# One-core delta-rule, Mish and Sinkhorn-gated expert kernel: the queue order of the first expert's values, gating steps and token sums is rewritten

## The chip, the cores and the metric

The kernel runs on one core of a Trainium2 chip. The metric is the device time of one execution in microseconds (us), the median of the runs of a kernel. Five engines have instruction queues of their own and run them in order: PE (TensorE, matrix products into PSUM), DVE (VectorE), ACT (ScalarE), POOL (GpSimd) and SP (SyncE, which here issues every DMA). An instruction that has to wait holds up all that stands behind it on its engine.

## The reference, cut to what matters

Three stages follow each other. A delta-rule attention gives 3072 tokens of 384 values. A gated MLP (Mish) follows. The last stage, to which the change belongs, is a dense mixture of eight experts, whose gates `P` are normalised by eight Sinkhorn rounds over all tokens:

```python
logits = x @ w_gate
P = np.exp(logits - logits.max())
for _ in range(8):
    P /= P.sum(1, keepdims=True) + 1e-09
    P /= P.sum(0, keepdims=True) + 1e-09
    P *= N / E
for e in range(E):
    h = np.maximum(x @ w1[e], 0.0)
    out += P[:, e:e + 1] * (h @ w2[e])
```

## The kernel before, in words

**Two phases.** Phase 1 walks six blocks of 512 tokens and does attention, the MLP and expert 0 for each. Phase 2 does experts 1 to 7. Its unit is a pair (e, i, g): expert e, token block i (0 to 5), group g of 256 hidden units (0 to 3). There are 7 x 6 x 4 = 168 pairs; pair p = 0 to 23 are those of expert 1, the first in phase 2 ("the first expert" of the change). Values are split into a high and a low part, so each product is three matmuls.

**What a pair does.** `first(p)` (matmuls L487) forms seven small products of the 128x256 quarters of x and w1 (a Strassen-like scheme) in four PSUM tiles: `b0` and `b2` from a pool of two ("h"), `b1` and `b3` from another pool of two ("a"), 3, 9, 9 and 12 matmuls in this order. `evacuate(p)` combines them: ACT copies `b0` (L509), DVE adds (L510 to L513, out of `b1`, `b2`, `b2`, `b3`), ACT applies the ReLU (L514), DVE forms the low part (L515). `second(p)` (24 matmuls, L1348) multiplies by w2 and adds into four PSUM tiles `o`; after the fourth group DVE multiplies `o` by the gate and adds it to the token sums `acc` (L1353). PE's order is first(0), first(1), second(0), first(2), second(1) and so on, so one pair's evacuation has a whole pair of matmuls to hide behind. A PSUM tile is written again only when its last reader has finished: `b1` of pair p+1 takes the place of what used "a" two tiles ago.

**What is prepared beside it, in the pairs of expert 1.** (1) The values of the next token block: `x_fetch` brings them from DRAM into the one buffer `gxr` (SP, L449), `x_begin` forms the four differences that the scheme needs (DVE, L456 to L459), three `x_split` calls make the high part (ACT, L465) and the low part (POOL, L466) in one of two buffers `gx`, and `x_store` writes them to DRAM for the later experts (SP, L469, tile `xcd`, 2.3 MB). (2) The weights: `g_load` forms sums (DVE, L432 to L435) and splits (ACT L437, POOL L439), then has the next ones fetched (SP, L412 and L416). (3) The Sinkhorn rounds: a `sink_step` is half a round. `sink_round` is five DVE instructions (L353 to L357); `sink_round_end` is one matmul (L361) into a PSUM tile taken from the pool "a", and four DVE instructions (L363 to L366). Fourteen of the 22 steps run in phase 1; eight are left for phase 2. (4) The token sums: expert 0's result, which phase 1 left in DRAM (`y0d`), is loaded into `acc` (SP, L1369) and multiplied by expert 0's gate (DVE, L1407), four instructions for each block, which can only start when all Sinkhorn steps are done.

**What sets the order.** The order on each engine is that of the Python loop over p (L1374 to L1407): first, evacuate, two sink steps, second of the pair before, two sink steps, `g_load` at p = 1 and 5 in expert 1, then one piece of the next block's values (`x_begin` at g = 0, a split at g = 1, 2 and 3, with fetch, store and the load of the sums of block i + 2 behind the last split), and at the end two multiplications of token sums.

Of the kernel before, what the change touches and what calls it, by code (L numbers as in the profile page):

```python
# [13 lines left out]
ALU = mybir.AluOpType  # L14
# [70 lines left out]
def delta_mish_sinkhorn_kernel(  # L85
# [16 lines left out]
    nc = tc.nc  # L102
# [226 lines left out]
    P = lg  # L329
# [42 lines left out]
    def sink_step():  # L372
        if sinks:
            sinks.popleft()()
# [4 lines left out]
    NGR = U2 // 2  # L379
# [3 lines left out]
    order = list(range(NBLK))  # L383
# [60 lines left out]
    def x_fetch(i):  # L444
        if i >= NBLK:
            return
        c = order[i]
        r = pool2["xr"].tile([128, NX, 256], F32, tag="xr", name="gxr")
        nc.sync.dma_start(out=r[:, 0:6].rearrange("p a x -> p (a x)"), in_=x2_dram[c].rearrange("p k x -> p (k x)"))  # L449
        xraw[i] = r  # L450
# [11 lines left out]
    def x_split(i, k):  # L462
        r, x = xraw[i], xq[i]
        s = slice(3 * k, 3 * k + 3)
        nc.scalar.activation(out=x[:, 0, s], in_=r[:, s], func=AF.Copy)  # L465
        nc.gpsimd.tensor_tensor(out=x[:, 1, s], in0=r[:, s], in1=x[:, 0, s].bitcast(F32), op=ALU.subtract)  # L466

    def x_store(i):
        nc.sync.dma_start(out=xc_dram[order[i]], in_=xq[i].bitcast(F32))  # L469
# [8 lines left out]
    def first(p):  # L478
        e, i, g = pairs[p]
        w, x = gslots[gslot(p)], xq[i]  # L480

        def prod(ps, *terms):
            last = 3 * len(terms) - 1
            n = 0
            for a, b in terms:
                for pw, px in PASSES:
                    mm(ps, lhsT=w[:, pw, a * 128:a * 128 + 128], rhs=x[:, px, b, :], start=(n == 0), stop=(n == last))  # L487
                    n += 1

        b0 = ps_h.tile([128, 512], F32, tag="h", name="b0")  # L490
        prod(b0[:, 0:256], (0, 0))
        b1 = ps_a.tile([128, 512], F32, tag="a", name="b1")
        prod(b1[:, 256:512], (7, 7))
        prod(b1[:, 0:256], (2, 2), (4, 4))
        b2 = ps_h.tile([128, 512], F32, tag="h", name="b2")
        prod(b2[:, 0:256], (8, 8))
        prod(b2[:, 256:512], (6, 6), (5, 5))
        b3 = ps_a.tile([128, 512], F32, tag="a", name="b3")
        prod(b3[:, 0:256], (3, 1), (5, 4))
        prod(b3[:, 256:512], (1, 3), (9, 5))  # L500
        fbanks[p] = [b.rearrange("p (a x) -> p a x", a=2) for b in (b0, b1, b2, b3)]
# [25 lines left out]
    if True:  # L527
# [708 lines left out]
        with tc.manual_schedule():  # L1236
            banks[:] = [0, [A1, A1]]
            for c in range(NBLK):
                pe, rest, late = window(c)
                if c == NBLK - 1:  # L1240
                    p1.close()
                    open_second()
                    rest["s1"].append(g_fetch)
                    rest["s1"].append(lambda: x_fetch(0))
                    for f in (5, 9, 13):
                        rest[f"s{f}"].append(g_load)
                    rest["s7"].append(lambda: x_begin(0))
                    for k, f in enumerate((8, 10, 11)):
                        rest[f"s{f}"].append(lambda k=k: x_split(0, k))
                    rest["s15"].append(lambda: x_store(0))  # L1250
                    rest["s15"].append(lambda: x_fetch(1))
                m0 = PLACES[0][0]
                b = c * NU

                def side_pe(m, part):
                    return [st() for st in (pe[m][2:] + late[m] if part else pe[m][:2])]

                def side_rest(m, posts):
                    for p in posts:
                        p()  # L1260
                    for r in rest[m]:
                        r()
                    for p in side_pe(m, 1):
                        p()

                rate(0.4 if c == 0 else 0.6)
                for f in range(U1 + 3):
                    m = MARKS[f]
                    posts = side_pe(m, 0)
                    if f < U1:  # L1270
                        ready(b + f)
                        m_first(b + f)
                    if 1 <= f <= U1:
                        m_a(b + f - 1)
                        m_c(b + f - 1)
                    if not c and f < m0:
                        elim1(10, nc.gpsimd)
                    if f == 0 and c:
                        y0_second(b - 1)
                    if f == 1 and c:  # L1280
                        y0_done(c - 1)
                    if f == 2 or not c:
                        banks[1] = [A1, A1, (ps_o1, "o3")]
                    if f == U1 + 1:
                        m_second(b + U1 - 1)
                        x2_done(c)
                    side_rest(m, posts)
                    if 2 <= f <= U1:
                        m_second(b + f - 2)
                    fill(2.0)  # L1290
                    if f < U1:
                        if not c:
                            decodes(min(U1, f + 4))
                            converts(min(U1, f + 3))
                            begins(min(U1, f + 5))
                        if ncvt[0] >= U1:
                            conversions(b + f)
                side_rest("f4", side_pe("f4", 0))
                fill(2.0)
                banks[1] = [A1, A1]  # L1300
                for f in range(U1, NU):
                    u = b + f
                    posts = side_pe(f"s{f}", 0)
                    ready(u)
                    e_first(u, ps_h, mi_p, x1h, x1l)
                    if f > U1:
                        e_relu(u - 1)
                    side_rest(f"s{f}", posts)
                    if f > U1:
                        fill(3.6 if c == 0 else 3.2)  # L1310
                    if c == NBLK - 1 and f > U1:
                        sink_step()
                        sink_step()
                    if f > U1 + 1:
                        y0_second(u - 2)
                    conversions(u)
                e_relu(b + NU - 1)
                split = [lambda kc=kc: st_x1(c + 1, kc) for kc in range(KD)] if c + 1 < NBLK else []
                if split:
                    run(*split[0:2])  # L1320
                y0_second(b + NU - 2)
                if split:
                    run(split[2])
            y0_second(NBLK * NU - 1)
            y0_done(NBLK - 1)
# [36 lines left out]
    with tc.manual_schedule():  # L1362
        N = len(pairs)
        todo = deque((c, t) for c in order for t in range(4))

        def acc_load(i):
            if i < NBLK:
                have[0] = i + 1
                nc.sync.dma_start(out=acc[order[i]], in_=y0_dram[order[i]])  # L1369

        have = [0]

        acc_load(0)
        acc_load(1)  # L1374
        for p in range(N + 1):
            if p < N:
                e, i, g = pairs[p]
                first(p)
                evacuate(p)
                sink_step()  # L1380
                sink_step()
            if p >= 1:
                second(p - 1)
                sink_step()
                sink_step()
                if pairs[p - 1][1] == NBLK - 1 or p in (1, 5):
                    g_load()
            if p < N:
                if e == 1 and i + 1 < NBLK:
                    if g == 0:  # L1390
                        x_begin(i + 1)
                    elif g < NGR - 1:
                        x_split(i + 1, g - 1)
                    else:
                        x_split(i + 1, 2)
                        x_fetch(i + 2)
                        x_store(i + 1)
                        acc_load(i + 2)
                elif g == 0 and p + NGR < N:
                    x_load(p + NGR)  # L1400
            if not sinks and todo:
                for _ in range(2):
                    if not todo or order.index(todo[0][0]) >= have[0]:
                        break
                    c, t = todo.popleft()
                    a = acc[c][:, t, :]
                    nc.vector.tensor_scalar(out=a, in0=a, scalar1=P[:, 4 * c + t, 0:1], scalar2=None, op0=ALU.mult)  # L1407


# [61 lines left out]
```

## Time and profile before

| | |
|---|---|
| median of 3 runs | 2378.32 us (2370.19, 2378.47, 2378.32) |
| the profiled execution | 2370.12 us, its span 2368.3 us |
| PE busy | 2254.5 us, 95% of the span |
| DVE / ACT / POOL busy | 52% / 26% / 22% |
| mean granted clock of TensorE | 0.969 of full speed |
| phase 2 | from 950.2 us to the end, 168 pairs |

The span is the profile's time from the first instruction to the last; the execution's own time is 1.8 us longer. PE is busy nearly everywhere, so the places where it isn't are what a change of order can touch. Below, a line of a timeline reads: start in us, length in us, engine, line, instruction, output<-input, shapes, how many were merged, and in brackets the idle time before and what ended it.

### The profile page before, as it was taken

What the parts mean: (1) busy time and instruction counts of PE and PEld (TensorE: products, weight loads), DVE (VectorE), ACT (ScalarE), POOL (GpSimd) and SP (SyncE); (2) the same over time, 40 slices, a digit from 0 to 9 for tenths busy, and PEclk for the clock granted to TensorE, in tenths of its full rate; (3) what the DMA queues carried; (4) which work ended last, traced back from release to release, by engine and by line L of the source; (5) the groups of instructions that cost most, each with busy time, mean ns of one, the idle gap of its engine ahead of it and who ended that gap; (6) DMA issues with size and microseconds to landing.
All of it is one profiled execution on the core that took longest, in us unless ns stands there. A gap on an engine that the chain in (4) does not pass through costs nothing.

```text
span 2368.3 us, 41965 instructions
## 1 busy us (share of the span) xinstructions
PE 2254.5 (95%) x18012; PEld 2084.9 (88%) x18012; DVE 1236.1 (52%) x2009; ACT 619.7 (26%) x1012; POOL 529.4 (22%) x439
## 2 busy tenths in 40 slices
PE   6698899999999999897999999999999999999998
PEld 3477778888888878897999999999999999999998
DVE  8875725427172123764555555555555555555554
ACT  5244332333323232221321221121122122112111
POOL 5586441331412051131300020030020002002000
PEclk7799999999999999998999999999999999999999
DMA  5367643637344565332231232222213113221321
GB/s 173 114 208 219 206 150 130 207 121 241 132 151 164 173 230 195 121 105 109 108 143 45 81 134 81 80 86 89 81 67 145 47 77 133 81 80 68 107 84 51
DMA packets 74441, 297.04 MB, mean 125 GB/s; under 512 B 7504, under 2 KB 39504, under 8 KB 68880
## 3 DMA queue, kind: packets, MB, share of 16 engines
q1 hardware_dynamic: 74256, 294.36, 36.0%
q8 instruction: 142, 2.33, 0.4%
q14 instruction: 43, 0.35, 0.0%
HBM read 247.15 MB, written 47.19 MB: 124 GB/s over the span
## 4 chain that ended last, share of the span: by engine, by line
issue 35%; PE 10%; DMA 5%; POOL 4%; DVE 1%; SPq 0%; ACT 0%; POOLq 0%; DVEq 0%; ACTq 0%
PE o L1348 5%; PE b L487 5%; DMA gr<-in_w_dram 4%; POOL gw L439 2%; POOL gx L439 1%; DMA acc<-y0d 1%; SPq L412 0%; POOL gx L466 0%; DVE acc L1353 0%; ACT gh L514 0%; DVE gt L510 0%; DVE gt L513 0%; ACT gw L437 0%; DVE gt L511 0%; DVE acc L1407 0%
## 5 line engine op out<-in xcount | busy, mean ns | idle before, releaser
L487 PE MATMUL b<-gx,gw 128*128 128x256 f32 x3564 | 452.5, 284 | 17.7 <-DVE gt L510 12.4
L487 PEld LDWEIGHTS b<-gx,gw 128*128 128x128 f32 x3564 | 444.2, 192 | 22.5 <-DVE gt L510 14.1
L1348 PE MATMUL o<-gw,gh 128*128 128x384 f32 x1728 | 443.0, 337 | 2.1 <-DVE acc L1353 2.1
L514 ACT ACTIVATE gh<-gt 128x1024 fp32r<-128x1024 f32 x168 | 178.3, 1061 | 647.2 <-DVE gt L513 647.2
L1348 PEld LDWEIGHTS o<-gw,gh 128*128 128x128 f32 x1728 | 309.7, 190 | 2.6 <-issue 2.6
L296 PE MATMUL psh<-xh,w 128*128 128x512 f32 x864 | 289.0, 416 | 23.2 <-DMA w<-wd 12.9
L515 DVE SCALAR_TENSOR_TENSOR gl<-gt,gh 128x1024 fp32r<-128x1024 f32 x168 | 209.6, 1247 | 189.4 <-ACT gh L514 189.4
L1348 PE MATMUL o<-gw,gl 128*128 128x384 f32 x864 | 291.1, 337 | 0.0
L510 DVE TENSOR_TENSOR gt<-b,gt 128x512 f32<-128x512 f32 x168 | 116.2, 691 | 302.0 <-PE b L487 238.1
L1348 PE MATMUL o<-gx,gh 128*128 128x384 f32 x960 | 247.5, 339 | 2.4 <-DVE acc L1353 2.4
L487 PE MATMUL b<-gx,gx 128*128 128x256 f32 x1980 | 243.7, 280 | 0.8 <-ACT gt L509 0.6
L487 PEld LDWEIGHTS b<-gx,gx 128*128 128x128 f32 x1980 | 240.4, 188 | 2.2 <-ACT gt L509 1.2
L296 PEld LDWEIGHTS psh<-xh,w 128*128 128x128 f32 x864 | 160.8, 195 | 65.1 <-issue 19.1
L978 POOL TENSOR_TENSOR gl<-x,gh 128x512 fp32r<-128x512 f32 x96 | 128.7, 1340 | 394.1 <-ACT gh L977 393.8
L439 POOL TENSOR_TENSOR gw<-gr,gw 128x512 fp32r<-128x512 f32 x72 | 90.8, 1293 | 561.4 <-ACT gw L437 561.4
L296 PE MATMUL psh<-xl,w 128*128 128x512 f32 x432 | 176.0, 407 | 4.2 <-DVE xl L607 4.2
L1348 PEld LDWEIGHTS o<-gx,gh 128*128 128x128 f32 x960 | 171.6, 188 | 2.9 <-issue 2.0
L1348 PEld LDWEIGHTS o<-gw,gl 128*128 128x128 f32 x864 | 163.6, 189 | 0.4
L1348 PE MATMUL o<-gx,gl 128*128 128x384 f32 x480 | 162.7, 339 | 0.0
L509 ACT ACTIVATE gt<-b 128x256 f32<-128x256 f32 x168 | 64.2, 382 | 352.2 <-PE b L487 328.9
L989 PE MATMUL x<-gh,w 128*128 128x512 f32 x576 | 150.0, 396 | 0.0
L439 POOL TENSOR_TENSOR gx<-gr,gx 128x512 fp32r<-128x512 f32 x40 | 50.4, 1294 | 440.9 <-ACT gx L437 440.9
(182 smaller groups left out, 2992.2 us busy)
## 6 DMA issues: line engine op xcount, KB each, us to landing
w<-wd SPq DMA_DIRECT2D x120, 768.0 KB, 4.6
gx<-xcd SPq DMA_DIRECT2D x36, 2304.0 KB, 9.0
gr<-in_w_dram SPq DMA_DIRECT2D x56, 384.0 KB, 3.6
wd<-w SPq DMA_DIRECT2D x24, 768.0 KB, 4.7
xcd<-gx SPq DMA_DIRECT2D x6, 2304.0 KB, 11.0
kq<-in_qkb_dram SPq DMA_DIRECT2D x20, 256.0 KB, 7.0
vt<-in_vtok_dram SPq DMA_DIRECT2D x6, 768.0 KB, 8.3
kq<-in_w_in_dram SPq DMA_DIRECT2D x12, 384.0 KB, 4.7
```

The lines of the kernel that those rows point to most:

```text
L296: mm(ps, lhsT=wi(u, pw, kc), rhs=(xh, xl)[px][:, kc, :], start=(n == 0), stop=(n == 3 * KD - 1))
L439: nc.gpsimd.tensor_tensor(out=w[:, 1, q:q + 512], in0=r[:, q:q + 512], in1=w[:, 0, q:q + 512].bitcast(F32), op=ALU.subtract)
L487: mm(ps, lhsT=w[:, pw, a * 128:a * 128 + 128], rhs=x[:, px, b, :], start=(n == 0), stop=(n == last))
L509: nc.scalar.activation(out=t[:, 7], in_=b0[:, 0], func=AF.Copy)
L510: tt(out=t[:, 0:7:6], in0=b1, in1=t[:, 7:8].to_broadcast([128, 2, 256]), op=ALU.add)
L514: nc.scalar.activation(out=h, in_=t[:, 0:4], func=AF.Relu)
L515: nc.vector.scalar_tensor_tensor(out=l, in0=t[:, 0:4], scalar=0.0, in1=h.bitcast(F32), op0=ALU.max, op1=ALU.subtract)
L978: nc.gpsimd.tensor_tensor(out=l, in0=p, in1=h.bitcast(F32), op=ALU.subtract)
L989: mm(x2ps[c][k], lhsT=wo(u, pw, k * 128, k * 128 + 128), rhs=(h, l)[pg], start=(f == 0 and n == 0), stop=(f == U1 - 1 and n == 2))
L1348: mm(o[t], lhsT=(h, l)[ph][:, z, (t % 2) * 128:(t % 2) * 128 + 128], rhs=w[:, pw, at:at + DM], start=(g == 0 and fi == 0 and n == 0), stop ...
```

## The change

The rounds, products and sums stay the same; nothing is left out of the computation. In the loop over the pairs:

- The two sink steps of a pair stand in front of `first(p)` instead of behind `evacuate(p)`, and the two behind `second(p - 1)` are gone. The eight steps take pairs 0 to 3 instead of 0 to 2.
- The multiplications of token sums stand behind `evacuate(p)`, four at a time: block 0 at pair 3, block 1 at pair 4, blocks 2 to 5 at pairs 6, 9, 12 and 15, each a pair or more ahead of the pair whose L1353 (L1352 now) adds to them.
- The loads of the token sums are issued one for each pair (`acc_load(p + 1)` at p = 1 to 4) instead of one for each block behind `x_store`.
- Of the next block's values, `x_begin` and the first split are issued at g = 1, the other two splits and the fetch at g = 2, the store at g = 3. Block 0's store moves from phase 1 to pair 2.

```diff
-                    rest["s15"].append(lambda: x_store(0))
                     rest["s15"].append(lambda: x_fetch(1))
...
                 e, i, g = pairs[p]
+                sink_step()
+                sink_step()
                 first(p)
                 evacuate(p)
-                sink_step()
-                sink_step()
+            for _ in range(4):
+                if sinks or not todo or p < 3 * order.index(todo[0][0]):
+                    break
+                c, t = todo.popleft()
+                a = acc[c][:, t, :]
+                nc.vector.tensor_scalar(out=a, in0=a, scalar1=P[:, 4 * c + t, 0:1], scalar2=None, op0=ALU.mult)
             if p >= 1:
                 second(p - 1)
-                sink_step()
-                sink_step()
+                acc_load(p + 1)
                 if pairs[p - 1][1] == NBLK - 1 or p in (1, 5):
                     g_load()
             if p < N:
+                if p == 2:
+                    x_store(0)
                 if e == 1 and i + 1 < NBLK:
-                    if g == 0:
+                    if g == 1:
                         x_begin(i + 1)
-                    elif g < NGR - 1:
-                        x_split(i + 1, g - 1)
-                    else:
+                        x_split(i + 1, 0)
+                    elif g == 2:
+                        x_split(i + 1, 1)
                         x_split(i + 1, 2)
                         x_fetch(i + 2)
+                    elif g == 3:
                         x_store(i + 1)
-                        acc_load(i + 2)
...
-            if not sinks and todo:
-                for _ in range(2):
-                    if not todo or order.index(todo[0][0]) >= have[0]:
-                        break
-                    c, t = todo.popleft()
-                    a = acc[c][:, t, :]
-                    nc.vector.tensor_scalar(out=a, in0=a, scalar1=P[:, 4 * c + t, 0:1], scalar2=None, op0=ALU.mult)
```

How DVE's queue stands between the evacuations of pairs 0 and 1, before (`gate`, `lg` are the Sinkhorn data, `gxr` the raw values of the next block, `gt` and `gl` an evacuation's tiles):

```order
L357 TENSOR_REDUCE gate<-lg 128x8
L456 TENSOR_TENSOR gxr<-gxr 128x256
L457 TENSOR_TENSOR gxr<-gxr 128x256
L458 TENSOR_TENSOR gxr<-gxr 128x256
L459 TENSOR_TENSOR gxr<-gxr 128x256
L510 TENSOR_TENSOR gt<-b_8716,gt 128x2x256
L511 TENSOR_TENSOR gt<-b_8726,gt 128x512
```

Two sink steps and `x_begin` stood in front of pair 1's evacuation. Now `x_begin` and the sums of `g_load` stand behind it, in front of the sink steps of pair 2:

```order
L513 TENSOR_TENSOR gt<-b_8741,gt 128x512
L515 SCALAR_TENSOR_TENSOR gl<-gt,gh 128x1024
L432 TENSOR_TENSOR gr<-gr 128x128
L433 TENSOR_TENSOR gr<-gr 128x256
L434 TENSOR_TENSOR gr<-gr 128x128
L435 TENSOR_TENSOR gr<-gr 128x128
L456 TENSOR_TENSOR gxr<-gxr 128x256
L457 TENSOR_TENSOR gxr<-gxr 128x256
L458 TENSOR_TENSOR gxr<-gxr 128x256
L459 TENSOR_TENSOR gxr<-gxr 128x256
L363 TENSOR_SCALAR gate<-psa 128x8
L364 RECIPROCAL gate<-gate 128x8
```

The L363 at the end reads the PSUM tile `psa` of pair 2's sink matmul; PE's last product of pair 2 takes that tile's place in the pool.

SP's queue at the start of phase 2, before (`acc` are the token sums, `xcd` a stored block of values, `gxr` a fetched one, `gr` raw weights):

```order
L1369 DMA acc_8637<-y0d_73 128x1536
L1369 DMA acc_8638<-y0d_74 128x1536
L412 DMA gr<-in_w_dram 128x3x256
L416 DMA gr<-in_w_dram 128x2x384
L449 DMA gxr<-x2d_81 128x1536
L469 DMA xcd_116<-gx 128x4608
L1369 DMA acc_8639<-y0d_75 128x1536
L412 DMA gr<-in_w_dram 128x3x256
```

and now:

```order
L1367 DMA acc_8636<-y0d_73 128x1536
L1367 DMA acc_8637<-y0d_74 128x1536
L1367 DMA acc_8638<-y0d_75 128x1536
L412 DMA gr<-in_w_dram 128x3x256
L416 DMA gr<-in_w_dram 128x2x384
L1367 DMA acc_8639<-y0d_76 128x1536
L469 DMA xcd_115<-gx 128x4608
L449 DMA gxr<-x2d_81 128x1536
L1367 DMA acc_8640<-y0d_77 128x1536
L469 DMA xcd_116<-gx 128x4608
L1367 DMA acc_8641<-y0d_78 128x1536
```

All six loads of token sums are issued before the third block's values are stored, and the store of block 0 (`xcd_115`) is now among them.

## Rows read from the trace of the kernel before

**Rows 1.** Busy time by stretch: busy us of PE, PEld, DVE, ACT, POOL; clock; DMA.

```profile
1050.00:1100.00 50.00, 42.78 (x288) 42.37 (x287) 24.44 (x39) 11.96 (x16) 9.97 (x5) 0.93 0.22 80
...
1200.00:1250.00 50.00, 50.00 (x355) 50.00 (x354) 27.72 (x39) 9.47 (x14) 0.00 (x0) 1.00 0.34 133
```

**Rows 2.** What PE waited for, 950 to 1160 us: total, times, longest.

```profile
PE b L487 <- DVE gt L510: 12.4, 2, 6.6
...
PE b L487 <- POOL gx L466: 2.1, 2, 1.5
```

**Rows 3.** Timeline of PE, pairs 0 to 5 (x33 is one first).

```profile
950.19 4.11 PE L487 MATMUL b<-gx,gw 128*128 128x256 f32 x33
...
962.27 0.60 PE L361 MATMUL psa<-gate 128*128 128x8 f32 x2 [3.06 <-DVE gt L510]
...
969.84 4.20 PE L487 MATMUL b<-gx,gw 128*128 128x256 f32 x33
977.26 0.39 PE L361 MATMUL psa<-gate 128*128 128x8 f32 x2 [3.23 <-DVE gt L510]
...
983.33 4.04 PE L487 MATMUL b<-gx,gx 128*128 128x256 f32 x33
...
999.89 4.12 PE L487 MATMUL b<-gx,gw 128*128 128x256 f32 x33
```

**Rows 4.** Timeline of PE, firsts of pairs 13, 14, 15, 17, 18.

```profile
1067.41 0.52 PE L487 MATMUL b<-gx,gw 128*128 128x256 f32 x3
1074.53 5.32 PE L487 MATMUL b<-gx,gw 128*128 128x256 f32 x30 [6.60 <-DVE gt L510]
1083.84 4.11 PE L487 MATMUL b<-gx,gw 128*128 128x256 f32 x33
1091.96 4.04 PE L487 MATMUL b<-gx,gx 128*128 128x256 f32 x33
...
1108.52 0.52 PE L487 MATMUL b<-gx,gw 128*128 128x256 f32 x3
...
1124.44 4.11 PE L487 MATMUL b<-gx,gw 128*128 128x256 f32 x33
```

**Rows 5.** Timeline of DVE, start of phase 2 and the wait in pair 12.

```profile
950.39 0.56 DVE L607 COPY xr<-y 128x384 f32<-128x384 f32 x1 [0.48 <-PE y L318]
...
957.30 0.16 DVE L363 TENSOR_SCALAR gate<-psa 128x8 f32<-128x8 f32 x1
...
960.07 0.42 DVE L456 TENSOR_TENSOR gxr<-gxr 128x256 f32<-128x256 f32 x1
...
961.53 0.68 DVE L510 TENSOR_TENSOR gt<-b,gt 128x512 f32<-128x512 f32 x1
...
965.19 1.23 DVE L515 SCALAR_TENSOR_TENSOR gl<-gt,gh 128x1024 fp32r<-128x1024 f32 x1 [1.12 <-ACT gh L514]
...
972.82 0.29 DVE L432 TENSOR_TENSOR gr<-gr 128x128 f32<-128x128 f32 x1
...
980.18 2.33 DVE L515 SCALAR_TENSOR_TENSOR gl<-gt,gh 128x1024 fp32r<-128x1024 f32 x1 [1.12 <-ACT gh L514]
...
982.86 1.38 DVE L365 TENSOR_SCALAR gate<-gate 128x8 f32<-128x8 f32 x1
...
1073.12 0.75 DVE L1407 TENSOR_SCALAR acc<-acc,lg 128x384 f32<-128x384 f32 x2 [15.15 <-DMA acc<-y0d]
```

**Rows 6.** Timeline of POOL, 974 to 985 us.

```profile
974.67 4.98 POOL L439 TENSOR_TENSOR gx<-gr,gx 128x512 fp32r<-128x512 f32 x4 [69.61 <-ACT gx L437]
979.60 4.62 POOL L466 TENSOR_TENSOR gx<-gxr,gx 128x768 fp32r<-128x768 f32 x2
```

**Rows 7.** Timeline of SP's queue: the load of block 4's token sums.

```profile
1060.53 0.43 SPq L1369 DMA_DIRECT2D acc<-y0d  x1
```

**Rows 8.** The page's DMA issues: count, KB each, median us to landing.

```profile
xcd<-gx SPq DMA_DIRECT2D x6, 2304.0 KB, 11.0
```

**Rows 9.** Timeline of PE, last block of phase 1.

```profile
916.92 1.19 PE L296 MATMUL psh<-xh,w 128*128 128x512 f32 x2 [0.65 <-DMA w<-wd]
```

More of the change, by code (lines that the diff above doesn't have):

```diff
@@ L1367, in acc_load @@
             if i < NBLK:
-                have[0] = i + 1
                 nc.sync.dma_start(out=acc[order[i]], in_=y0_dram[order[i]])
-        have = [0]
         acc_load(0)
@@ L1388, in delta_mish_sinkhorn_kernel @@
             if p < N:
+                if p == 2:
+                    x_store(0)
                 if e == 1 and i + 1 < NBLK:
-                    if g == 0:
+                    if g == 1:
                         x_begin(i + 1)
-                    elif g < NGR - 1:
-                        x_split(i + 1, g - 1)
-                    else:
+                        x_split(i + 1, 0)
+                    elif g == 2:
+                        x_split(i + 1, 1)
                         x_split(i + 1, 2)
                         x_fetch(i + 2)
+                    elif g == 3:
                         x_store(i + 1)
-                        acc_load(i + 2)
                 elif g == 0 and p + NGR < N:
                     x_load(p + NGR)
-            if not sinks and todo:
-                for _ in range(2):
-                    if not todo or order.index(todo[0][0]) >= have[0]:
-                        break
-                    c, t = todo.popleft()
-                    a = acc[c][:, t, :]
-                    nc.vector.tensor_scalar(out=a, in0=a, scalar1=P[:, 4 * c + t, 0:1], scalar2=None, op0=ALU.mult)
+        assert not sinks and not todo
 def _layout(inp):
```

## The prediction

> **What bounds the kernel now.** I read the busy times by stretch first, to see where PE isn't at work. From 1200 to 1250 us, in the pairs of expert 2, PE is busy 50 of 50 us at the full granted clock, while between 1050 and 1100 it is busy 42.8 and the clock is granted at 0.93 [rows 1]. So the kernel is bound by PE, except in the pairs of expert 1, and only these does the change touch. The waits of PE say on what: 12.4 us in two waits of a product for L510, DVE's first addition, and 2.1 us for POOL's splits [rows 2]. The timeline of PE then gives the price of each place. An undisturbed pair takes 8.12 us (1083.84 to 1091.96) [rows 4], of which a first is 4.11 [rows 3]. Against that, between the firsts of neighbouring pairs:
>
> Pair 1 (about 954.3, right behind the first of 950.19) to 2: 15.5 us, 7.4 lost. Pair 2 to 3: 13.5, 5.4 lost. Pairs 3 to 5: 16.6 for two, 0.3 lost [rows 3]. Pairs 5 to 13: 67.5 for eight, 2.6 lost, of which 2.1 are POOL's [rows 2 to 4]. Pair 13 to 14: 16.4, 8.3 lost. Pairs 14 to 17: 24.7 for three, 0.3 lost. Pair 17 to 18: 15.9, 7.8 lost [rows 4]. Together 32.1 us, and there are two causes.
>
> The first is DVE's order at the start. The two waits of 3.06 and 3.23 us at L361 [rows 3] are waits for a PSUM tile: the sink matmul takes a tile of pool "a" behind `b1`, and DVE reaches `b1` only after two sink steps (957.30 to 960.07, 2.77 us) and `x_begin` (to 961.53, 1.46) [rows 5]. The second is the load of token sums. Block 4's was issued at 1060.53 [rows 7] and DVE stood at its multiplication for 15.15 us until 1073.12 [rows 5], which is 12.6 us after the issue; pair 12's evacuation was queued behind it, and PE stopped in pair 13 after three matmuls for 6.60 us [rows 4]. The 30 matmuls behind this wait took 5.32 us; 33 of them take 4.11 elsewhere. Block 5's load does the same in pair 17.
>
> **The change part by part.** *Sink steps in front of a pair.* DVE is now free of phase 1 at 950.95 [rows 5] and does the steps of pair 0 at once. From there it is a chain without gaps worth counting: a pair costs it 2.77 for the steps and 4.89 for the evacuation (961.53 to the end of L515 at 966.42) [rows 5], 7.66 in sum, less than PE's 8.12. After two pairs, at 966.3, come the sums of `g_load` (four instructions such as 0.29 at 972.82, about 1.15) and `x_begin` (1.46). So L363 of pair 2 begins at 950.95 + 15.3 + 2.6 = 968.9. PE's last twelve matmuls of pair 2 need the PSUM tile that L363 frees; without that wait they would stand at about 967.2, so some 1.9 us are lost there, and about 1.8 more in pair 1 (its `b1` waits for L513 of pair 0, which the sink steps pushed back). From 969.1, twelve matmuls (12/33 of 4.11, 1.5), second(1) (8.12 less 4.11, about 4.15) and the next sink matmul bring the first of pair 3 to 974.9, against 983.33 [rows 3]: 8.4 gained. Pair 3's DVE chain (one half step and an evacuation) ends at 950.95 + 3 x 7.66 + 2.6 + 1.0 + 4.9 = 982.4, and second(3) wants it only at 987. From there on PE sets the pace; pairs 3 to 5 give 0.3 more. Sum of this part: 8.7.
>
> *What it puts beside POOL.* Before, the sink steps up to 972.8 ran while POOL did nothing; its work began at 974.67 [rows 6], 1.85 after L432 [rows 5]. Now L432 stands at 966.3, so POOL works from about 968.1 for 4.98 + 3 x 2.31 = 11.9 us, right through pair 2's sink steps. Beside POOL, L515 took 2.33 us instead of 1.23, and L365, an instruction of 8 columns, 1.38 (its sister L363 took 0.16) [rows 5, 6]. Pair 2's steps have two TENSOR_SCALARs from SBUF, up to one POOL instruction (4.98/4 = 1.25) each: 0 to 2.5. One of `x_begin`'s four sums may wait (0 to 1.2) and L515 of pair 2 may be stretched (0 to 1.1). Of 4.8 at most, about 0.8 is slack of PE. Bounds 0 and 4, and 6.5 if the two TENSOR_TENSORs of the rounds (L366, L356) wait 1.25 each too; nearest is the row of L365, so I take 3.
>
> The Trainium skill's page "SBUF — State Buffer" (Who interferes with whom) says that DVE and GpSimd hold a shared port pair as an exclusive lock, and that a DVE instruction with two SBUF inputs also contends with a GpSimd instruction that reads SBUF. The 2.33 us of L515, which has two, agrees. By that rule L366 and L356 would each wait for a POOL instruction as well, and the loss here is the 6.5 instead of 3; that is the second rival.
>
> *Token sums loaded early and multiplied a pair ahead.* The loads are issued in pairs 1 to 4. SP's queue there holds a fetch of weights (it waits for POOL to finish with `gr`, near 973), the store of block 0, a fetch of values (it waits for the splits of pair 2, POOL done at about 980 to 983) and the store of block 1. So the last load is issued near 990 and, at the 12.6 us seen, landed by 1003. Block 5's sums are wanted in pair 15, twelve pairs of 8.12 behind 974.9, at about 1072. Block 0's and 1's are loaded before pair 1. Both DVE waits that stopped PE go, and with them 8.3 and 7.8. What is late next there? Four multiplications (0.75 for two [rows 5], 1.5 a pair) stand behind an evacuation of 4.89: 6.4 of 8.12, so DVE keeps up.
>
> *Values pair by pair.* In a pair with g = 1, DVE does 4.89 + 1.46 and ACT one split more; the next L509 comes at about the time PE has `b0` ready. The splits are done at g = 2, two pairs before the block is used, so the 2.1 us for POOL go; of the 2.6 lost in pairs 5 to 13 I take 1.8. The splits write a buffer of `gx` that the store of two blocks back has to have left: block 0's store issued at about 975 lands near 986 (11.0 [rows 8]) and is wanted at about 1001. The 0.3 in pairs 14 to 17 I count as 0.3. This part and the one before: 8.3 + 7.8 + 1.8 + 0.3 = 18.2.
>
> *The store out of phase 1.* A wait of 0.65 us for weights [rows 9] came while that store was still in the DMA queues. Bounds 0 and 2 (the half clock behind it); I take 0.7.
>
> *Clock.* Behind the 6.60 us wait PE lost about 1.6 more at a lower granted clock [rows 4]. The waits that stay at the start are of 1 to 3 us, two of them near that size: 0 to 4, I take 1.5.
>
> Sum: 8.7 + 18.2 + 0.7 - 3.0 - 1.5 = 23.1 us. The profiled execution took 2370.1 us (span 2368.3), so 2347.0. Of the three runs shown, one is at that level and two are 8.2 us higher (median 2378.3); no row tells which level the changed kernel takes. At the upper one it is 2355.2. I name the middle, 2351.
>
> **Rivals.** *The steps lose more beside POOL.* Two additional waits in pair 2's rounds, 6.5 in place of 3: the gain is 19.6, the time 2350.5 or 2358.7, middle 2354.6. For it: L515 and L365 in the rows. Against it: L510 to L513, with one SBUF input, have not been seen stretched.
>
> *The waits for token sums only move.* If SP reaches the loads of blocks 3 to 5 late, because it stands at the fetches in between, DVE stops again, one pair earlier than PE can hide. The gain is then the 8.7, 1.8 and 0.7 less 4.5: 6.7, and the time 2363.4 or 2371.6, middle 2367.5. Against it: there are some 65 us between the last load's landing and its use.
>
> *Slower.* ACT stands at the first split of a block until the store of two blocks back has left the buffer, and L509 of the next pair is queued behind it, so PE stops as it did for DVE. It happens for four blocks (2 to 5). It begins to cost when a store lands more than about 26 us after its issue (11 by the row and 15 of slack), and it decides once each of the four lands 9 us after that: 4 x 9 = 36 eats the gain of 23 and 12 more. The time is then 2351 + 36 = 2387. For it: the store shares the queues with four loads and a fetch that were spread out before. Against it: the row's 11 us is under half of the 26.
>
> **How the numbers follow.** Forecast 0.64, beside POOL 0.22, moved waits 0.09, slower 0.05. The low end is all of 8.7, 19.0 and 2 gained with nothing lost: 2340. The high end is 6.5 and 4 lost and nothing from phase 1, 16.4 gained at the upper level, 2362, and two us towards the moved waits: 2364. A measurement of this kernel can tell about 0.5% from no change, 12 us, so faster means under 2366.4: the first two cases and half of the third, 0.91. Within 0.5%: the other half and a mild case of the last, 0.06. Slower: 0.03.
>
> **What the profile would show.** Right: no wait of DVE for `acc`; PE's waits for L510 gone from pairs 12 to 18; the first of pair 3 between 974 and 981 and of pair 18 some 23 to 28 us before 1124.44; a wait of 2 to 3 us in pair 2 for L363. Wrong: firsts of pairs 5 to 20 more than 8.2 us apart, ACT idle at L465 for a DMA, L366 or L356 over 1 us in pair 2. The forecast fails if the DVE chain of pairs 0 to 3 is longer than 32 us, or if phase 1 differs by more than 2 us.

## The result, and the profile after

The changed kernel took 2347.4 us (median of 4 runs, 2342.8 to 2351.1), against 2374.9 us before in the same comparison (4 runs, 2370.2 to 2378.5): a ratio of 0.9884 with a 95% interval of 0.9854 to 0.9914. The profiled execution took 2351.13 us with a span of 2349.4.

Busy time by stretch of the changed kernel (columns as in [rows 1]: busy us of PE, PEld, DVE, ACT, POOL, granted clock, DMA):

```profile
950.00:1000.00 50.00, 45.74 (x303) 44.65 (x302) 40.20 (x76) 12.89 (x18) 11.20 (x7) 0.97 0.57 208
1000.00:1050.00 50.00, 50.00 (x355) 50.00 (x355) 38.41 (x64) 15.35 (x21) 15.11 (x9) 1.00 0.29 109
1050.00:1100.00 50.00, 50.00 (x355) 50.00 (x355) 31.41 (x52) 10.87 (x15) 8.36 (x5) 1.00 0.36 127
```

The stretch from 1050 to 1100, in which PE had been busy 42.8 of 50 us [rows 1], is now full and at the full granted clock; only the first 50 us of phase 2 have holes left. What PE waited for there (total, times, longest), 940 to 1160 us:

```profile
PE b L487 <- DVE gate L363: 2.5, 1, 2.5
PE b L487 <- DVE gt L513: 1.7, 2, 1.0
```

The 12.4 us for L510 and the 2.1 for POOL [rows 2] are gone, and so are the two waits at L361 [rows 3]. What is left is DVE's chain in pairs 1 to 3. The timeline of PE shows it, answering to [rows 3, 4]:

```profile
955.14 4.20 PE L487 MATMUL b<-gx,gw 128*128 128x256 f32 x33
...
961.07 4.13 PE L487 MATMUL b<-gx,gw 128*128 128x256 f32 x30 [1.01 <-DVE gt L513]
...
974.57 2.33 PE L487 MATMUL b<-gx,gw 128*128 128x256 f32 x12 [2.48 <-DVE gate L363]
...
983.26 4.12 PE L487 MATMUL b<-gx,gx 128*128 128x256 f32 x30 [0.70 <-DVE gt L513]
991.41 4.11 PE L487 MATMUL b<-gx,gw 128*128 128x256 f32 x33
...
1072.65 4.11 PE L487 MATMUL b<-gx,gw 128*128 128x256 f32 x33
...
1105.11 4.11 PE L487 MATMUL b<-gx,gw 128*128 128x256 f32 x33
```

The last three rows are the firsts of pairs 4, 14 and 18: from pair 4 on 14 pairs take 113.7 us, 8.12 each, which is the undisturbed pair. Behind the 2.48 us wait the last twelve matmuls of pair 2 ran long (2.33 us, where 12/33 of 4.11 are 1.5), and so did the start of `second(1)`: the granted clock was 0.66 from 974.57 to 976.90 and 0.81 from there to 981.80.

Phase 1 hides part of this: in this profile the first of pair 0 stands at 955.14 instead of 950.19. So kernels are compared below by the time from the first of pair 0 to the first of pair 4 and of pair 18, read from the same timeline. It repeats to 0.1 us in the three profiles whose phase 2 is that of the changed kernel (changed, changed again, store in phase 1).

| kernel | first of pair 0 at | to pair 4 | to pair 18 | median of runs |
|---|---|---|---|---|
| before | 950.19 | 41.18 | 174.25 | 2374.9 |
| changed | 955.14 | 36.27 | 149.97 | 2347.4 |
| changed, again | 953.58 | 36.22 | 149.92 | 2344.6 |
| before + loads early | 942.16 | 42.09 | 158.48 | 2354.2 |
| before + late multiplications | 956.07 | 40.90 | 155.94 | 2354.7 |
| changed, steps behind | 948.92 | 40.46 | 154.17 | 2347.4 |
| changed, values as before | 951.94 | 33.05 | 154.25 | 2351.1 |
| changed, store in phase 1 | 954.29 | 36.18 | 149.88 | 2347.4 |
| changed, pair 2's steps first | 953.06 | 35.26 | 148.97 | 2344.9 |
| changed, no steps in pair 2 | 952.54 | 32.35 | 147.97 | 2344.5 |

The medians belong to three comparisons, in which the kernel before had 2374.9, 2373.3 and 2371.6 us. Against it, the changed kernel and its variants have ratios from 0.9879 to 0.9913, with 95% intervals that overlap, so the runs do not tell them apart. Only the times to pair 4 and to pair 18 do, with one profile for each variant. Nor are these always good to 0.1 us: the kernel before and its two variants have the same order on PE and DVE up to pair 4 and reach it after 41.18, 42.09 and 40.90, since PE's waits at L361 were followed by different granted clocks (below). A difference of 1 us between two rows is not shown to come from an edit.

The change is worth 24.3 us by pair 18 (174.25 less 149.97). Behind pair 18 nothing moved: 1243.9 us to the end of the span before (2368.3 - 950.19 - 174.25), 1244.3 after.

How DVE stands in pairs 0 to 3 of the changed kernel, answering to [rows 5]:

```profile
955.68 0.16 DVE L363 TENSOR_SCALAR gate<-psa 128x8 f32<-128x8 f32 x1
...
958.48 0.68 DVE L510 TENSOR_TENSOR gt<-b,gt 128x512 f32<-128x512 f32 x1
...
963.92 0.36 DVE L366 TENSOR_TENSOR lg<-lg,gate 128x192 f32<-128x192 f32 x1
...
973.07 1.37 DVE L459 TENSOR_TENSOR gxr<-gxr 128x256 f32<-128x256 f32 x1
974.36 0.15 DVE L363 TENSOR_SCALAR gate<-psa 128x8 f32<-128x8 f32 x1
...
975.65 1.40 DVE L366 TENSOR_TENSOR lg<-lg,gate 128x192 f32<-128x192 f32 x1
...
978.60 1.60 DVE L356 TENSOR_TENSOR lg<-lg,gate 128x192 f32<-128x192 f32 x1
...
980.67 0.68 DVE L510 TENSOR_TENSOR gt<-b,gt 128x512 f32<-128x512 f32 x1
...
987.32 1.95 DVE L366 TENSOR_TENSOR lg<-lg,gate 128x192 f32<-128x192 f32 x1
```

Two steps take 2.80 us in pair 0 (955.68 to 958.48) and 6.31 in pair 2 (974.36 to 980.67). POOL's timeline in the same stretch, answering to [rows 6]:

```profile
972.72 5.47 POOL L439 TENSOR_TENSOR gx<-gr,gx 128x512 fp32r<-128x512 f32 x4 [60.67 <-ACT gx L437]
978.15 1.82 POOL L466 TENSOR_TENSOR gx<-gxr,gx 128x768 fp32r<-128x768 f32 x1
985.10 3.94 POOL L466 TENSOR_TENSOR gx<-gxr,gx 128x768 fp32r<-128x768 f32 x2 [5.12 <-ACT gx L465]
```

Pair 2's steps lie beside it up to their last reduction, and so does the half round of pair 3 (L366 1.95 us at 987.32). The RECIPROCALs and the TENSOR_REDUCE L353 among them kept their length (0.20, 0.30 and 0.35 us).

### The profile page after: what moved, and what is told of

It reads as the page before. It is cut to its first block, busy times and chain, and to the rows that moved or that the text cites. A ratio compares the mean times of both kernels' runs of the same rounds, so it can differ in the third digit from the quotient of the medians.

```text
span 2349.4 us, 41970 instructions
## 1 busy us (share of the span) xinstructions
PE 2262.2 (96%) x18012; PEld 2090.3 (89%) x18012; DVE 1239.3 (53%) x2009; ACT 619.7 (26%) x1012; POOL 527.3 (22%) x439
## 3 DMA queue, kind: packets, MB, share of 16 engines
q8 instruction: 142, 2.33, 0.4%
## 4 chain that ended last, share of the span: by engine, by line
PE 51%; issue 30%; DVE 7%; DMA 5%; POOL 5%; SPq 1%; ACT 1%; POOLq 0%; DVEq 0%; ACTq 0%
PE psh L296 12%; PE o L1347 11%; PE b L487 10%; PE x L989 8%; PE y L318 3%; DMA gr<-in_w_dram 3%; POOL gw L439 2%; DVE t L784 1%; DVE lane L790 1%; DMA w<-wd 1%; POOL gx L439 1%; PE psa L739 1%; PE psa L878 1%; PE psa L912 1%; DVE lane L772 1%
## 5 line engine op out<-in xcount | busy, mean ns | idle before, releaser
L515 DVE SCALAR_TENSOR_TENSOR gl<-gt,gh 128x1024 fp32r<-128x1024 f32 x168 | 207.7, 1236 | 189.4 <-ACT gh L514 189.4
L510 DVE TENSOR_TENSOR gt<-b,gt 128x512 f32<-128x512 f32 x168 | 116.2, 691 | 309.6 <-PE b L487 245.3
```

What stands on the lines that cost most here:

```text
L510: tt(out=t[:, 0:7:6], in0=b1, in1=t[:, 7:8].to_broadcast([128, 2, 256]), op=ALU.add)
L515: nc.vector.scalar_tensor_tensor(out=l, in0=t[:, 0:4], scalar=0.0, in1=h.bitcast(F32), op0=ALU.max, op1=ALU.subtract)
```

## The experiments

**Loads of the token sums early, nothing else** (kernel before as base):

```diff
                 second(p - 1)
+                if p <= 4:
+                    acc_load(p + 1)
...
                         x_store(i + 1)
-                        acc_load(i + 2)
```

> The kernel before with one edit: the loads of token sums for blocks 2 to 5 are issued in pairs 1 to 4. Measured inside phase 2, from the first of pair 0 (before: pair 4 starts 41.2 us later, pair 18 174.3 us later; changed kernel 36.3 and 150.0). Theory (the two stops in pairs 13 and 17 are DVE standing at a load issued too late): pair 4 unchanged at 41.2, pair 18 at about 158 (16.1 less), total about 16 us faster than before. Rival (it is the place of the multiplications behind an evacuation that stops PE, not the load): pair 18 stays near 174, total unchanged.

Pair 18 stands at 158.48, 15.8 less than before; the runs give 0.9932 (0.9904 to 0.996). The firsts of pairs 13, 14 and 18 in its timeline of PE:

```profile
1059.71 4.12 PE L487 MATMUL b<-gx,gw 128*128 128x256 f32 x33
1067.84 4.11 PE L487 MATMUL b<-gx,gw 128*128 128x256 f32 x33
...
1100.64 4.11 PE L487 MATMUL b<-gx,gw 128*128 128x256 f32 x33
```

Pair 13 to 14 takes 8.13 us where it took 16.4 [rows 4]. So the load's time of issue was the cause of both stops; the rival falls. Pair 4 was expected unchanged at 41.2 and came at 42.09: behind the wait of 3.24 us at L361 the granted clock was 0.58 for 7.25 us, where before it was 0.72 for 6.07.

**Multiplications late, loads as before** (kernel before as base):

```diff
-                    if not todo or order.index(todo[0][0]) >= have[0]:
+                    if not todo or order.index(todo[0][0]) >= have[0] or p < 4 * order.index(todo[0][0]):
```

> The kernel before with one edit: loads of token sums stay where they were, but each block's multiplications wait until the pair in which that block begins (pair 4c for block c), four or more pairs behind the load for blocks 2 to 5. Theory (DVE stops only because it is sent to the data before they landed): as with early loads, pair 18 at about 158, total about 16 us faster. Rival (a late load costs by itself, through the queues it shares with the stores): pair 18 at 162 or more.

Pair 18 at 155.94, 18.3 less than before, and 0.9921 (0.9894 to 0.9949). Late loads cost nothing by themselves here: what stopped PE was DVE, sent to data that had not landed, with an evacuation queued behind. That this gains 2.5 us more than early loads was not expected. Of it, 1.2 lie in front of pair 4 (42.09 against 40.90) and are the clock's. The rest is PE's wait for POOL at pair 8, 1.4 us, which early loads left and which is gone here, though the splits stand where they stood. The traces show why: two multiplications that stand beside POOL's splits take three times their length. In the kernel before it is 2.34 us (1017.51), where two take 0.75 elsewhere [rows 5], and with early loads 2.33 (1010.38). Pair 7's evacuation is queued behind them on DVE, its ReLU on ACT waits for it, and the third split is queued behind the ReLU: so with early loads it starts 7.16 us after the first of pair 7 (1016.16). With late multiplications none stand there, and it starts after 5.76 (1027.49).

**The changed kernel again**, unedited:

> The changed kernel once more, unedited. Theory (phase 1 differs from run to run by some us whatever the kernel, phase 2 repeats): pair 4 at 36.3 and pair 18 at 150.0 us behind the first of pair 0 to within 0.3; the first of pair 0 anywhere from 947 to 956 us; time 2343 to 2351. Rival (the 5 us by which phase 1 was longer in the changed kernel's profile come from the change): the first of pair 0 at 955 again.

Pair 4 at 36.22 and pair 18 at 149.92, as in the first profile; first of pair 0 at 953.58, 2344.6 us (2341.4 to 2348.4). Over the ten profiles of this study that first stands anywhere from 942.16 to 956.07, with no order by kernel. The changed kernel's profile was already 7.6 us behind the other when phase 1's fifth block stored its values (804.98 against 797.40), before any instruction that the change touches. So the 5 us by which phase 1 was longer are a difference between executions.

**Pair 2's steps in front of pair 1's weight sums** (changed kernel as base):

```diff
-                sink_step()
-                sink_step()
+                if p != 2:
+                    sink_step()
+                    sink_step()
                 first(p)
...
                 acc_load(p + 1)
+                if p == 1:
+                    sink_step()
+                    sink_step()
```

> The changed kernel with one edit: the two sink steps of pair 2 stand in front of pair 1's weight sums and values instead of behind them, so that DVE does them before POOL starts. Theory (L366 and L356 took 1.4 and 1.6 us in pair 2 because POOL was working beside them): both back to 0.36, PE's 2.48 us wait for L363 gone, a new wait of up to 3 us in pair 3 for the weights that POOL now makes later; pair 4 at 34 to 35 instead of 36.3. Rival (they are slowed by the DMAs that land then): L366 and L356 stay above 1 us. Total 1 to 2 us faster than the changed kernel, too little for a verdict.

The steps of pair 2 ran before POOL's work (from 973.44 there) and L366 is short; the half round of pair 3 ran beside it and L366 is long. Two rows of its timeline of DVE, and one of PE:

```profile
969.43 0.36 DVE L366 TENSOR_TENSOR lg<-lg,gate 128x192 f32<-128x192 f32 x1
...
983.41 1.94 DVE L366 TENSOR_TENSOR lg<-lg,gate 128x192 f32<-128x192 f32 x1
```

```profile
977.11 0.39 PE L361 MATMUL psa<-gate 128*128 128x8 f32 x2 [1.49 <-DVE gt L510]
978.97 5.35 PE L487 MATMUL b<-gx,gx 128*128 128x256 f32 x30 [0.85 <-DVE gt L513]
```

The wait for L363 is gone, as expected. L356 took 0.36 us as well (970.76). The price was misjudged: pair 4 at 35.26, not 34 to 35. The new wait in pair 3 is there, but for DVE and not for the weights: `x_begin` and the evacuation of pair 2 now come late, PE waits 1.49 and 0.85 us, and the thirty matmuls behind these take 5.35 us instead of 4.12, at a granted clock of 0.68. Pair 18 is 1.0 us earlier than in the changed kernel, too little to count. On the rival: in pair 1 of the changed kernel, while three loads of token sums issued from 959.22 were under way (the DMA engines were busy at 0.99 from 961 to 965), L366 took 0.36 us (963.92). DMAs landing don't stretch it; POOL's work does.

**Steps behind, as before** (changed kernel as base):

```diff
-                sink_step()
-                sink_step()
                 first(p)
                 evacuate(p)
+                sink_step()
+                sink_step()
...
                 second(p - 1)
+                sink_step()
+                sink_step()
                 acc_load(p + 1)
```

> The changed kernel with its sink steps put back where they were: two behind an evacuation and two behind the second of the pair before; token sums and values stay as changed. Theory (at the start DVE is one chain of work and PE follows it, so the place of the steps in front of a pair is worth some us): pair 4 at 38.5 to 39.5 us behind the first of pair 0, between 36.2 (changed) and 41.2 (before); two waits of PE at L361 for L510 of 2 us or more are back; pair 18 at about 152.5. Rival (the steps in front of a pair are worth nothing, the gain at the start comes from the values alone): pair 4 at 36.3.

Pair 4 at 40.46 and pair 18 at 154.17, 4.2 more than changed. Its waits at the sink matmuls in the timeline of PE:

```profile
959.53 0.39 PE L361 MATMUL psa<-gate 128*128 128x8 f32 x2 [1.60 <-DVE gt L510]
966.59 0.36 PE L361 MATMUL psa<-gate 128*128 128x8 f32 x2 [2.41 <-DVE gate L357]
...
975.27 0.39 PE L361 MATMUL psa<-gate 128*128 128x8 f32 x2 [4.26 <-DVE gt L510]
```

The place of the steps carries nearly all of the gain at the start, 1 to 2 us more than I expected of it. Of the two waits for L510 that I expected, at 2 us or more, one is 4.26 and the other only 1.60. The matmul at 966.59 shows a second mechanism: with four steps in a pair, PE also waits for the round itself (L357). In the kernel before, PE came to this matmul later: `second(0)`, behind the 3.06 us wait, ran at a granted clock of 0.58 there (962.27 to 969.84 [rows 3]).

**Values in their old places** (changed kernel as base):

```diff
-                    if g == 1:
+                    if g == 0:
                         x_begin(i + 1)
-                        x_split(i + 1, 0)
-                    elif g == 2:
-                        x_split(i + 1, 1)
+                    elif g < NGR - 1:
+                        x_split(i + 1, g - 1)
+                    else:
                         x_split(i + 1, 2)
                         x_fetch(i + 2)
-                    elif g == 3:
                         x_store(i + 1)
```

> The changed kernel with the values' pieces put back to one for each pair (differences at g = 0, a split at each of g = 1, 2, 3, fetch and store at g = 3); steps and token sums stay as changed. Theory (the third split then ends only when the next block's first products want it): PE waits for POOL at pairs 4, 8, 12, 16, 0.6 to 2.7 us each; pair 4 at 34 to 36.3 (fewer POOL instructions beside pair 2's steps), pair 18 2 to 6 us later than 150. Rival (with the token sums multiplied a pair ahead DVE is never late, and the old places do as well): no wait for POOL, pair 18 at 150 or less.

Pair 4 comes earlier, at 33.05: `x_begin` no longer stands in front of pair 2's steps, and these take 4.1 us (970.19 to 974.29) instead of 6.3, since less of POOL's work lies beside them. Pair 18 comes at 154.25, 4.3 later. So the new places cost 3.2 us at the start and bring 7.5 behind it. Waits for POOL are back at pairs 4 and 8:

```profile
987.81 5.11 PE L487 MATMUL b<-gx,gw 128*128 128x256 f32 x28 [1.69 <-POOL gx L466]
...
1024.77 3.62 PE L487 MATMUL b<-gx,gw 128*128 128x256 f32 x28 [1.69 <-POOL gx L466]
```

I had expected one at pairs 12 and 16 too, and there was none. The two blocks that pay are those whose splits share their pairs with weight sums; that these are the reason was not tested. The runs gave 2351.1 us (2350.0 to 2354.1).

**Block 0's store back in phase 1** (changed kernel as base):

```diff
+                    rest["s15"].append(lambda: x_store(0))
                     rest["s15"].append(lambda: x_fetch(1))
...
-                if p == 2:
-                    x_store(0)
```

> The changed kernel with block 0's store of values put back into phase 1. The last stretch of phase 1, from the store of block 5's x2 to the store of its expert-0 result, took 40.6 us before and 38.4 and 38.4 in two profiles of the changed kernel. Theory (the store's 2.3 MB held up the weights there): 40 us or more again, with a wait of PE for a weight load. Rival (a difference between runs): 38.4. Phase 2 as in the changed kernel: pair 4 at 36.3, pair 18 at 150.

The two stores on SP's queue that bound the last stretch of phase 1:

```profile
914.90 0.32 SPq L1002 DMA_DIRECT2D x2d<-xr  x1
...
954.97 0.32 SPq L959 DMA_DIRECT2D y0d<-xr  x1
```

That is 40.07 us. The six profiles without the store in phase 1 have 38.39 to 38.45; the four with it 38.81, 39.98, 40.07 and 40.57. So the stretch is 0.4 to 2.2 us longer with the store. The store does hold up the weights, as the theory has it: the weight load issued about 1 us behind it took 17.3 us to land in this profile and 16.0 in the three others with the store, where the load at the same place took 10.3 to 11.0 in the six without it. And PE waits here at the place of [rows 9], where the changed kernel has no wait:

```profile
922.76 0.70 PE L296 MATMUL psh<-xh,w 128*128 128x512 f32 x2 [1.44 <-DVE hl L311]
```

The profile puts this down to L311, which ended at 922.74, but the weight load issued at 905.32 landed at 922.6, so which of the two released PE is not shown. With early loads and with late multiplications PE has no wait there. Not all of the 2.2 need be the store's: the same stretch one block earlier, with no store in any kernel, took 38.2 us in eight profiles and 39.7 in two. Phase 2 didn't change.

**No steps in pair 2** (changed kernel as base):

```diff
-                sink_step()
-                sink_step()
+                if p != 2:
+                    sink_step()
+                    sink_step()
                 first(p)
```

> The changed kernel with one edit: no sink steps in pair 2, where POOL is at work; the steps take pairs 0, 1, 3 and 4. Theory (PE follows DVE's chain at the start, and the steps beside POOL cost 3.5 us more than alone): pair 4 at 33 instead of 36.3, PE's waits in pair 2 and 3 gone, pair 18 at 146.5 to 147.5; 3 us faster than the changed kernel. Rival (the steps only move their cost, since pairs 3 and 4 then carry it): pair 18 at 150.

Pair 4 at 32.35, better than expected; pair 18 at 147.97, 2.0 less than changed, worse than expected. The waits that are left, in its timeline of PE:

```profile
975.63 2.40 PE L487 MATMUL b<-gx,gx 128*128 128x256 f32 x18 [0.20 <-DVE gt L513]
978.53 1.68 PE L487 MATMUL b<-gx,gx 128*128 128x256 f32 x12 [0.50 <-DVE gate L363]
...
986.50 4.12 PE L487 MATMUL b<-gx,gw 128*128 128x256 f32 x30 [1.00 <-DVE gt L513]
```

PE's 2.48 us wait shrinks to 0.50, but pair 3's steps meet POOL's last splits, and pair 4 then pays 1.00 for the evacuation. Part of the cost moved on, so the rival had a third of it right. The runs (2344.5 us, 2337.1 to 2348.1) can't tell this kernel from the changed one; the 2.0 us are the profile's.

## Why the prediction was right, and where it was not

Point by point, between the first of pair 0 and that of pair 18:

- *Start, pairs 0 to 5:* forecast 8.7 less 3 for POOL and 1.5 for the clock, 4.2. Measured 49.70 - 44.45 = 5.3 (the first of pair 5 before and after), of which about 1 hangs on the clock that the kernel before happened to get. Putting the steps back costs 4.2.
- *Pairs 5 to 18:* forecast 18.2. Measured 124.55 - 105.52 = 19.0. The two stops at the token sums are 15.8 of it by the experiment with early loads; the old places of the values cost 4.3 in all. 15.8 + 4.2 + 4.3 = 24.3, the whole of the gain. That they add up so well is in part luck: the 15.8 were measured on the kernel before, the other two on the changed one, and with the late multiplications' 18.3 the sum would be 26.8.
- *Store:* forecast 0.7 with bounds 0 and 2; the stretch it stood in is 0.4 to 2.2 longer with it.
- *Sum:* forecast 23.1, measured 24.3 in phase 2 and 0.4 to 2.2 in phase 1. The medians of the runs differ by 27.5; the rest is within what phase 1 differs by between executions. The forecast time, 2351, was the middle of two levels seen before. The 16 later runs of the kernel before lie anywhere from 2363.8 to 2381.6, so there are no two levels but a spread. That the median came out at 2347.4, next to the 2347.0 of the lower level, is partly luck.

The step of the working that failed is the price of POOL's work beside the steps. I took 3 us because I let only the TENSOR_SCALARs of the steps wait. L366 and L356, with two SBUF inputs, waited too, 1.40 and 1.60 us against 0.36, so the second rival's condition came true. Its price didn't: the TENSOR_SCALARs waited less than a whole POOL instruction (0.83 us for L365 in pair 2), L515 of pair 2 was not stretched at all, and against that the half round of pair 3, which I had left out of this price, lost 2.7 (985.47 to 989.19, 3.7 us for what takes 1.0). DVE lost 3.5 in pair 2's steps, 1.0 in `x_begin` and 2.7 in pair 3, 7.2 in all. How much of it PE saw: without any such loss my chain put the first of pair 4 some 33 us behind pair 0's; it came at 36.27, 3.4 later with the low clock in it. About 1.6 of this is the clock: from 974.57 to 981.82 PE took 7.25 us for the twelve matmuls and `second(1)`, which by the sum in the prediction take 1.5 and 4.15. So some 1.8 is left for POOL, where I took 3, and the size of 4.5 for both was near by errors that cancel: DVE lost more than I counted, and PE saw less of it. The clock's 1.6 against 1.5 is luck as well, since the same waits were followed by different clocks in other profiles. The Trainium skill's page "SBUF — State Buffer" (Who interferes with whom) names an instruction with two SBUF inputs among those that contend with a GpSimd instruction that reads SBUF; L366 at 0.36 alone and 1.40, 1.94 and 1.95 beside POOL agrees.

The third rival (moved waits) was wrong by the clearest row: the last load of token sums was issued at 990.39 and no wait of DVE for `acc` is left.

```profile
990.39 0.67 SPq L1367 DMA_DIRECT2D acc<-y0d  x1
```

The slower rival found no trace either: ACT's splits never waited for a store.

Of the signs that were named, those for the token sums came out: no wait for `acc`, no wait of PE for L510 left, a wait of 2.48 us for L363 in pair 2, and pair 18 earlier by 24.3 (23 to 28 forecast) from the first of pair 0, though by only 19.3 on the profile's clock. The first of pair 3 stood at 981.96, outside 974 to 981; taken from the first of pair 0 it is 26.8 us, which on the time of the kernel before is 977.0. But three of the signs of being wrong came true too: L366 and L356 took over 1 us in pair 2, phase 1 differed by 5 us, and DVE's chain of pairs 0 to 3 took 38.4 us (955.68 to the end of L515 at 994.07), not under 32. The forecast held all the same. The median of several runs evens out much of phase 1's spread, and PE saw only part of the chain's delay: its end at 994.07 still came before `second(3)`, which started behind the first of 991.41 without a wait. So these two limits said less about the time than the prediction has it.

## What to carry to other kernels

Send an engine to data only when the data have landed: here a late load cost nothing by itself, but an in-order queue that stands at it holds up everything behind, in this kernel an evacuation and so TensorE. At a place where one engine's chain sets the pace, count what a second engine does beside it: small VectorE TENSOR_SCALARs out of SBUF and TENSOR_TENSORs with two SBUF inputs took up to eight times their length beside GpSimd's subtractions here (0.17 to 1.38 us, 0.36 to 1.95). Where execution times differ by more than the change, compare an interval inside the profile that repeats.

## What the runs showed that was not expected

- The time to phase 2 differs by 14 us between executions (942.16 to 956.07), in code that is the same in all ten kernels up to the last block; the interval behind it repeats to 0.1 us for the same kernel.
- TENSOR_SCALARs of 8 and 24 columns are as exposed to POOL's work as long ones: L365 took 0.17 us alone and 1.38 beside it, L354 0.18 and 0.76. RECIPROCALs of the same size were not.
- A wait alone doesn't say whether the granted clock falls. Of two waits of the same length, 1.69 us, one was followed by 28 matmuls in 5.11 us at a granted clock of 0.67 (987.81), the other by 28 in 3.62 at 1.00 (1024.77). The wait of 3.06 us at the sink matmul of pair 1 was followed by 0.58 in the kernel before (962.27) and by 1.00 with late multiplications (968.16). What decides is not shown.
